# Sliding-window attention and a phase-mixing layer on one core: the first loads on other queues, later loads in smaller pieces, a shifted order list

## The chip, the cores and the metric

One core of a Trainium2 chip runs the whole kernel. The metric is the device time of one execution in microseconds (us); the time before is the median of three runs. Engines are called as the profile calls them: PE (TensorE; PEld is its weight load), DVE (VectorE), ACT (ScalarE), POOL (GpSimd), SP (SyncE).

## What is computed

Attention with 8 heads over 4 batches of 768 positions; each position sees the first 8 positions and the 96 up to itself, with a bias by distance. Then a layer over positions and channels:

```python
scores = q @ k.T / 8 - slope[h] * dist          # masked to 8 global + 96 local positions
x = softmax(scores) @ v                         # heads side by side: 768 x 512 per batch
theta = x @ w_theta
y = w_tok_r @ (x * cos(theta)) + w_tok_i @ (x * sin(theta))
u = x + y
out = u + relu(u @ w_ch)
```

Inputs and the output are fp32 in HBM; inside, the operands of matmuls are bf16.

## The kernel before, in words

**Stages of a batch.** `attention(b, p)` takes two heads (pair p of 4). It turns q and k on PE (L450, 64x64 transposes, in the plan `tk`), untangles them out of PSUM (L459) and builds a second set of keys with the global positions (`copy_s`, L465 and L466). Scores come in three groups of 3, 4 and 4 blocks of 128 columns (L496). In batch 0 the bias by distance is added on PE by a matmul with a scaled identity (L489); in later batches it is a multiplication by exp(bias) after the exponential (L513, L518). Exponentials are on ACT (L504, or L507 where a group is split over two PSUM banks); values follow (L545), the norm (L554, L555), and x is turned (L571) and copied (L574). `theta(b)` is a matmul (L620), cosine and sine on ACT (L628, L631) and a product on DVE (L637, into `zri`). `mixing(b)` multiplies by both token matrices (L662) and adds x (L671). `channel(b)` turns u (L694), multiplies by w_ch (L698), copies u (L703), adds (L720) and stores by SP's queue (L725), the last half tile by ACT's. The token matrices are turned once by `turn_w` (L589, copies L593), between theta and mixing of batch 0, and the exp(bias) tables are made on ACT after the sines of batch 0 (L746).

**Loads.** All are issued by POOL, in one chain (`load`, `chain`), and convert fp32 to bf16 on the way: for batch 0 q, k and v of two heads at a time (`piece` L354, `piece_v` L359), with the position iota (L299) between the first pair's and the second's; then w_theta (L369), w_tok_r and w_tok_i whole (L377), batch 1 in three loads of eight heads each, w_ch (L372); batches 2 and 3 again three loads each, when the buffers are free. The natural token matrix w_tok_r lies in the buffer `zri[1]` until it is turned. Eight landing semaphores go round: the ninth load waits for the first to land. `spread_v` copies v to a second layout (`vs`, L396 and L400) on POOL, ACT or DVE.

**The order.** Each step is an entry with an engine (or several, of which the plan chooses one), a planned cost, its dependencies, the PSUM banks that it takes and frees, and a priority. `Plan.order` runs a greedy model of the engines: at each moment the ready step of lowest priority goes next. PE steps of 64-row matmuls (`tiled`) and full ones are told apart, with planned costs for going from one kind to the other (`INTO`, `BACK`). `HOP` is the planned delay from one engine to the next. The steps are then issued in that order; the chip keeps the order on each engine, but its times are its own. PSUM is two double banks and four single ones.

**Keeping PE busy.** `keep_up` issues matmuls on zeros (L324): 8 and then 5 at the start, 4 after the first transposes.

Of the kernel before, what the change touches and what calls it, by code (L numbers as in the profile page):

```python
# [11 lines left out]
FP = mybir.dt.float32  # L12
# [35 lines left out]
        self.end = None  # L48


HOP = {"PE": 0.28, "ACT": 0.18, "DVE": 0.18, "POOL": 0.25, "SP": 0.0, "DMA": 1.9, "STORE": 1.5}

INTO, BACK = 0.25, 0.17

WIDER = 1.0
AHEAD = 110
# [3 lines left out]
class Plan:  # L62
# [2 lines left out]

    def __init__(self, n_wide, n_narrow):
        self.steps = []
        self.hints = []
        self.n_wide = n_wide
        self.n_tiles = n_wide + n_narrow  # L70

    def add(self, *a, **k):
        s = Step(*a, **k)
        self.steps.append(s)
        return s
# [22 lines left out]
        return best  # L98

    def order(self):  # L100

        for seed, n, width, upto in self.hints:
            draw = random.Random(seed)
            for _ in range(n):
                self.steps[draw.randrange(upto or len(self.steps))].prio += draw.uniform(-width, width)
        users = {}
        left = {}
        for s in self.steps:
# [11 lines left out]
        tiled, into = False, INTO  # L120
# [20 lines left out]
        while len(done) < len(self.steps):  # L141
# [39 lines left out]
            s.eng = eng  # L181
            if eng == "PE":
                tiled = s.tiled
                into = 0.28 if s.dense else 0.13
            s.cost, s.emit = s.ways[eng][:2]
            cost = s.cost
            if s.table and s.table != table:
# [26 lines left out]
def kernel(  # L214
# [58 lines left out]
    xT = [sb.tile([T, NP, NT, T], BF, name=f"xT_{i}") for i in range(2)]  # L273
    cs_t = [sb.tile([T, 2, 2, DM], BF, name=f"cs_{i}") for i in range(3)]
    zri = [sb.tile([T, NT, 2, DM], BF, name=f"zri_{i}") for i in range(2)]
    uT = [sb.tile([T, NP, S], BF, name=f"uT_{i}") for i in range(2)]
    un_t = [sb.tile([T, DM], BF, name=f"un_{i}") for i in range(4)]
    o_t = [sb.tile([T, DM], FP, name=f"o_{i}") for i in range(4)]
# [6 lines left out]
    ]  # L285

    plan = Plan(N_WIDE, N_NARROW)
    add = plan.add
    ANY = list(range(N_WIDE + N_NARROW - 1, -1, -1))

# [27 lines left out]
    def keep_up(n, cost, deps, prio):  # L318

        bk = Bank(False, ANY)  # L320

        def fn():
            for _ in range(n):
                nc.tensor.matmul(narrow(bk), lhsT=nought[:, 0:T], rhs=nought, start=True, stop=True)  # L324
        add("PE", n * cost, fn, deps, prio, takes=bk, frees=[bk], dense=True)

    s_nought = add("DVE", 0.2, c_nought, [], -60)
    keep_up(8, 0.43, [s_nought], -60)
    keep_up(5, 0.215, [s_nought], -59)
    s_ones = add("DVE", 0.5, c_zero, [], -50)  # L330
    s_iota = Step("POOL", 0.37, c_iota, [], -1000)
    s_ident = add("DVE", 0.12, c_ident, [s_iota], -48)
    s_dist = add("DVE", 0.9, c_dist, [s_iota], -29)
    s_W, s_I = {}, {}
    for h in range(H):
        def c_i(copy, h=h):
# [9 lines left out]
    def load(cost, fn, deps=(), issue=0.75):  # L346
        deps = list(deps) + chain[-1:] + (landed[-8:-7] if len(landed) >= 8 else [])
        i = add("POOL", issue, fn, deps, -1000)
        chain.append(i)
        landed.append(add("DMA", cost, lambda: None, [i], len(landed)))  # L350
        return landed[-1]

    def piece(src, dst, b, h0, n):
        nc.gpsimd.dma_start(  # L354
            out=dst[b % 2][:, h0:h0 + n, :, :].rearrange("p h t d -> p h (t d)"),
            in_=src[b, h0:h0 + n].rearrange("h (p t) d -> p h (t d)", p=T))

    def piece_v(b, h0, n):
        nc.gpsimd.dma_start(  # L359
            out=v_t[b % 2][:, h0:h0 + n, :, 0:D].rearrange("p h t d -> p (h t) d"),  # L360
            in_=v[b, h0:h0 + n].rearrange("h (t p) d -> p (h t) d", p=T))

    s_q, s_k, s_v, s_vs = {}, {}, {}, {}
    att_end = {}
    s_w = {}

    def weights(name):
        if name == "th":
            fn = lambda: nc.gpsimd.dma_start(out=w_th, in_=moe_w_theta.rearrange("(c p) n -> p c n", p=T))  # L369
            s_w[name] = load(2.6, fn)  # L370
        elif name == "ch":
            fn = lambda: nc.gpsimd.dma_start(out=w_ch, in_=moe_w_ch.rearrange("(c p) n -> p c n", p=T))  # L372
            s_w[name] = load(2.6, fn)
        else:
            wi = int(name)
            src = (moe_w_tok_r, moe_w_tok_i)[wi]
            fn = lambda: nc.gpsimd.dma_start(out=w_nat[wi], in_=src.rearrange("(c p) n -> p c n", p=T))  # L377
            s_w[name] = load(6.0, fn)

    def copies(eng):  # L380
        return {"POOL": nc.gpsimd.tensor_copy, "DVE": nc.vector.tensor_copy, "ACT": nc.scalar.copy}[eng]
# [1 line left out]
    def any_of(fn, deps, prio, ways, **k):  # L383

        made = {e: (c, (lambda e=e: fn(copies(e))), d) for e, (c, d) in ways.items()}
        first = next(iter(made))
        s = add(first, made[first][0], made[first][1], deps, prio, other=made, **k)
        return s
# [18 lines left out]
    def between(step):  # L407

        step.deps += chain[-1:]
        plan.steps.append(step)  # L410
        chain.append(step)

    def loads(b, h0, n, after):
        qi = load(0.5 * n, lambda: piece(q, q_t, b, h0, n), after)
        ki = load(0.5 * n, lambda: piece(k, k_t, b, h0, n), after)
        vi = load(0.8 * n, lambda: piece_v(b, h0, n), after, issue=0.62 + 0.21 * n)
        vs = spread_v(b, h0, n, [vi])
        for h in range(h0, h0 + n):
            s_q[b, h], s_k[b, h], s_v[b, h], s_vs[b, h] = qi, ki, vi, [vs[(h - h0) // 2]]

    for h in range(H):
        s_I[h] = any_of(s_I[h][0], [s_ident], s_I[h][1], {"ACT": (0.2, 0.0), "DVE": (0.12, 0.0)})
# [1 line left out]

    groups = [(0, 3), (3, 4), (7, 4)]
    po_apart = set()
    sc_apart = {(0, p, 2) for p in range(NP)}
    on_pe = {(0, p, g) for p in range(NP) for g in range(3)}
    x_done, xT_done, exp_done = {}, {}, []
    att_log = {}  # L430
# [2 lines left out]
    def attention(b, p):  # L433
# [3 lines left out]
        kS3, e3, rc = kS[n % 3], ex[n % 3], rec[n % 2]  # L437
        kq3 = kq[n % 3]
        cold = 1.1 if n == 0 else 1.0
        old = att_log.get(n - 3, [None, None])  # L440
        bank = [Bank(False, ANY), Bank(False, ANY)]

        def turn():
            for which, src in enumerate((k_t, q_t)):
                for t in range(NT):
                    for r in range(2):
                        for hh in range(2):
# [2 lines left out]
                            nc.tensor.transpose(dst[:, c0:c0 + 64],  # L450
                                                src[b % 2][64 * r:64 * r + 64, h0 + hh, t, :],
                                                ident[64 * r:64 * r + 64, 64 * r:64 * r + 64])
        tk = add("PE", 0.4, turn, [s_k[b, h0], s_q[b, h0], s_ident, old[0]], pr + 10, takes=bank, tiled=True)
        if n == 0:
            keep_up(4, 0.215, [tk], 0)

# [5 lines left out]
        def copy_s(copy):  # L462
# [1 line left out]
            inner = inner.rearrange("p (r s) -> p r s", r=2)[:, :, 0:2 * T].rearrange("p r (t a) -> p r t a", t=2)  # L464
            copy(out=kS3.rearrange("p (r t) a -> p r t a", r=2)[:, :, :, G:T], in_=inner[:, :, :, G:T])  # L465
            copy(out=kS3[:, :, 0:G], in_=kq3[:, 0, 0:1, 0:G].to_broadcast([T, NT - 2, G]))  # L466
        both = {"DVE": (0.87, 0.0), "ACT": (0.72, 0.0)} if b or p < 1 else {"DVE": (0.87, 0.0)}
        kq0 = any_of(lambda copy: untangle(0, copy), [tk, old[0]], pr + 12, both, frees=bank[0:1])
        kq1 = any_of(lambda copy: untangle(1, copy), [tk, old[0]], pr + 12, both, frees=bank[1:2])
        cS = any_of(copy_s, [kq0, kq1], pr + 13, {"DVE": (0.5, 0.0), "ACT": (0.85, 0.1)})  # L470

        mult = []
        for g, (c0, n_c) in enumerate(groups):
            apart = (b, p, g) in sc_apart
            sc = [Bank(False, ANY), Bank(False, ANY)] if apart else [Bank(True, ANY)]
# [41 lines left out]
                    w = w[:, :, None, :].to_broadcast([T, 2, 2, 2 * T])  # L517
                    nc.vector.tensor_mul(dst, dst, w)  # L518
            need = [old[1]] + ([kq0] if g == 0 else [kq0, kq1, cS]) + ([s_dist, s_I[h0], s_I[h0 + 1]] if by_pe else [])
            s1 = add("PE", (0.057 + 0.107 * by_pe) * n_c * cold, scores, need, pr + 20 + g, takes=sc, tiled=True)  # L520
            s2 = add("ACT", 0.13 * len(sc) + 2 * n_c * T * 0.00076, exps, [s1, old[1]], pr + 30 + g, table="exp", frees=sc)
            if by_pe:
                s3 = s2
            else:
                s3 = add("DVE", 0.12 + 2 * n_c * T / 1960.0, weigh, [s2, s_W[h0], s_W[h0 + 1]], pr + 40 + g)
            mult.append(s3)
            last_s = s1

            exp_done.append(s2)

# [19 lines left out]
        def norm():  # L550
# [5 lines left out]
            else:  # L556
                for hh in range(2):
# [1 line left out]
                    nc.vector.reciprocal(rc[:, hh, :], ps[:, :, D])  # L559
                    nc.vector.tensor_mul(dst[:, hh, :, :], ps[:, :, 0:D],  # L560
                                         rc[:, hh, :, None].to_broadcast([T, NT, D]))
        att_log[n] = [last_s, last]
        nm = add("DVE", 0.85 + 0.3 * len(po), norm, [last] + [z_done[b - 2, st] for st in range(NT) if b >= 2], pr + 60, frees=po)
        x_done[b, p] = nm

# [7 lines left out]
        def copy_x(copy):  # L573
# [1 line left out]
                 in_=narrow(bk).bitcast(BF)[:, 0:S])  # L575
        t1 = add("PE", 0.34, turn_x, [nm], pr + 70, takes=bk)
        xT_done[b, p] = any_of(copy_x, [t1] + mix_log.get(b - 2, []), pr + 71,
                               {"DVE": (0.5, 0.0), "ACT": (0.7, 0.0)} if b or p == 3 else {"DVE": (0.5, 0.0)}, frees=[bk])
        att_end[b, p] = last

    def turn_w(wi, prio):
        got = []
        for st in range(NT):
            bk = Bank(False, ANY)

            def fn(st=st, bk=bk):
                ps = narrow(bk).bitcast(BF)
                for tt in range(NT):
                    nc.tensor.transpose(ps[:, tt * T:(tt + 1) * T],  # L589
                                        w_nat[wi][:, tt, st * T:(st + 1) * T], ident)  # L590

            def cp(copy, st=st, bk=bk):
                copy(out=wT[wi][:, st, :], in_=narrow(bk).bitcast(BF)[:, 0:S])  # L593
            t1 = add("PE", 0.35, fn, [s_w[str(wi)], s_ident], prio + st, takes=bk)
            got.append(any_of(cp, [t1], prio + st, {"DVE": (0.5, 0.0), "ACT": (0.72, 0.0)}, frees=[bk]))
        return got

# [130 lines left out]
            o_log.append(st)  # L728


    for h0 in (0, 2, 4, 6):
        loads(0, h0, 2, [])
        if h0 == 0:
            between(s_iota)
    weights("th")
    weights("0")
    weights("1")
    loads(1, 0, 8, [])
    weights("ch")
    for p in range(NP):  # L740
        attention(0, p)
# [9 lines left out]
    channel(0)  # L751
    for b in range(1, B):
        if b >= 2:
            loads(b, 0, 8, [att_end[b - 2, p] for p in range(NP)])
        for p in range(NP):
            attention(b, p)
        theta(b)
        mixing(b)
        channel(b)
# [38 lines left out]
```

## Time and profile before

| | us |
|---|---|
| median of three runs (lowest to highest) | 182.67 (182.27 to 183.24) |
| the profiled execution | 181.96 |
| its span | 180.0 |
| PE busy in the span | 167.9 |
| DVE, ACT, POOL busy | 124.2, 122.8, 35.9 |
| DMA queue of POOL: packets, MB | 35728, 12.85 |

The span goes from the first to the last instruction of the profiled execution; the rest of its time lies around it. Busy time counts instructions that run, so an engine's idle time in a stretch is the stretch less its busy time. The time from a load's issue to its landing is in the part on DMA issues: 5.6 and 6.4 us in the middle for q and k of two heads (192 KB in bf16), 21.7 and 24.1 us for eight heads (768 KB), 14.8 and 19.6 us for the token matrices (1152 KB).

### The profile page before, as it was taken

What the parts mean: (1) busy time and instruction counts of PE and PEld (TensorE: products, weight loads), DVE (VectorE), ACT (ScalarE), POOL (GpSimd) and SP (SyncE); (2) the same over time, 40 slices, a digit from 0 to 9 for tenths busy, and PEclk for the clock granted to TensorE, in tenths of its full rate; (3) what the DMA queues carried; (4) which work ended last, traced back from release to release, by engine and by line L of the source; (5) the groups of instructions that cost most, each with busy time, mean ns of one, the idle gap of its engine ahead of it and who ended that gap; (6) DMA issues with size and microseconds to landing.
All of it is one profiled execution on the core that took longest, in us unless ns stands there. A gap on an engine that the chain in (4) does not pass through costs nothing.

```text
span 180.0 us, 5292 instructions
## 1 busy us (share of the span) xinstructions
PE 167.9 (93%) x2311; PEld 101.6 (56%) x2325; DVE 124.2 (69%) x231; ACT 122.8 (68%) x189; POOL 35.9 (20%) x44
## 2 busy tenths in 40 slices
PE   7977979989699999999999999999999999999991
PEld 2434454766367666455666664656566555555560
DVE  1757955867898897788999964678679356524352
ACT  2697786999886885998979939948686990203010
POOL 7996930040530164006000000000000000000000
PEclk9999999999999999999999999999999999999998
DMA  4999999999999959992000210031001300400404
GB/s 55 144 179 185 210 210 209 204 187 150 203 204 165 191 81 207 179 182 100 4 0 4 108 71 2 4 134 46 0 4 58 117 4 0 162 13 4 174 0 175
DMA packets 39350, 19.47 MB, mean 108 GB/s; under 512 B 25376, under 2 KB 36384, under 8 KB 39328
## 3 DMA queue, kind: packets, MB, share of 16 engines
q0 software_dynamic: 35728, 12.85, 70.0%
q1 hardware_dynamic: 3456, 6.16, 9.5%
q8 instruction: 18, 0.29, 0.7%
q10 hardware_dynamic: 144, 0.13, 0.2%
q14 instruction: 4, 0.03, 0.1%
HBM read 25.69 MB, written 6.29 MB: 178 GB/s over the span
## 4 chain that ended last, share of the span: by engine, by line
PE 78%; ACT 7%; DMA 4%; POOL 3%; issue 3%; DVE 2%; DVEq 0%; POOLq 0%; ACTq 0%
PE ps L662 34%; PE ps L698 11%; PE ps L620 9%; PE ps L496 6%; PE ps L545 6%; DMA k<-in_k_dram 4%; PE ps L450 3%; PE ps L694 3%; PE ps L571 3%; ACT cs L628 2%; ACT ex L504 2%; PE ps L489 1%; POOL q L354 1%; POOL v L359 1%; ACT cs L631 1%
## 5 line engine op out<-in xcount | busy, mean ns | idle before, releaser
L662 PE MATMUL ps<-wT,zri 128*128 128x384 bf16 x384 | 69.1, 326 | 0.0
L662 PEld LDWEIGHTS <-zri 128*128 128x128 bf16 x384 | 35.1, 98 | 22.8 <-issue 0.9
L504 ACT ACTIVATE ex<-ps 128x1024 bf16<-128x1024 f32 (+1 forms) x44 | 40.5, 953 | 7.4 <-PE ps L496 7.3
L671 DVE TENSOR_TENSOR uT<-xT,ps 128x384 bf16<-128x384 bf16 x32 | 17.6, 551 | 17.8 <-PE ps L662 17.7
L703 ACT COPY un<-ps 128x512 bf16<-128x512 bf16 x18 | 10.7, 595 | 26.1 <-PE ps L694 26.0
L637 DVE TENSOR_TENSOR zri<-x,cs 128x1024 bf16<-128x1024 bf16 x24 | 16.5, 695 | 11.2 <-ACT cs L631 11.2
L698 PE MATMUL ps<-w_ch,uT 128*128 128x512 bf16 (+1 forms) x91 | 23.4, 370 | 0.5 <-issue 0.2
L459 DVE COPY kq<-ps 128x768 bf16<-128x768 bf16 x20 | 18.8, 952 | 5.5 <-PE ps L450 5.3
L620 PE MATMUL ps<-w_th,xT 128*128 128x512 bf16 x92 | 21.4, 379 | 0.2
L628 ACT ACTIVATE cs<-ps,halfpi 128x512 bf16<-128x512 f32 x24 | 17.4, 723 | 5.5 <-PE ps L620 5.4
L720 DVE SCALAR_TENSOR_TENSOR o<-ps,un 128x512 f32<-128x512 f32 (+1 forms) x25 | 16.6, 668 | 4.8 <-PE ps L698 4.4
L518 DVE TENSOR_TENSOR ex<-ex,Wm 128x1024 bf16<-128x1024 bf16 x24 | 16.5, 686 | 1.7 <-ACT ex L504 1.7
L545 PEld LDWEIGHTS <-ex 128*128 128x128 bf16 x352 | 13.7, 97 | 4.1 <-DVE ex L518 0.7
L496 PE MATMUL ps<-kq 64*128 64x128 bf16 (+1 forms) x192 | 15.1, 226 | 0.7 <-ACT ex L504 0.5
L555 DVE TENSOR_TENSOR x<-ps,rec 128x768 bf16<-128x768 f32 x16 | 15.3, 957 | 0.6
L620 PEld LDWEIGHTS <-xT 128*128 128x128 bf16 x96 | 9.2, 98 | 10.9 <-DVE xT L574 0.5
L545 PE MATMUL ps<-v,ex 128*128 128x65 bf16 x224 | 15.3, 193 | 0.0
L631 ACT ACTIVATE cs<-ps 128x512 bf16<-128x512 f32 x24 | 15.3, 638 | 0.0
L359 POOL DMA_DIRECT2D v<-in_v_dram x7 | 10.9, 1560 | 15.9 <-ACT wT L593 13.2
L574 ACT COPY xT<-ps 128x768 bf16<-128x768 bf16 x10 | 8.0, 799 | 7.8 <-PE ps L571 7.7
L396 POOL COPY vs<-v 128x520 bf16<-128x520 bf16 x9 | 6.4, 732 | 30.1 <-DMA v<-in_v_dram 30.1
L698 PEld LDWEIGHTS <-uT 128*128 128x128 bf16 x100 | 8.8, 98 | 6.1
(68 smaller groups left out, 207.0 us busy)
## 6 DMA issues: line engine op xcount, KB each, us to landing
out_dram<-o SPq DMA_DIRECT2D x23, 256.0 KB, 2.1
q<-in_q_dram POOLq DMA_DIRECT2D x3, 768.0 KB, 21.7
k<-in_k_dram POOLq DMA_DIRECT2D x3, 768.0 KB, 24.1
v<-in_v_dram POOLq DMA_DIRECT2D x3, 768.0 KB, 25.4
zri<-in_moe_w_tok_r_dram POOLq DMA_DIRECT2D x1, 1152.0 KB, 14.8
w_nat<-in_moe_w_tok_i_dram POOLq DMA_DIRECT2D x1, 1152.0 KB, 19.6
q<-in_q_dram POOLq DMA_DIRECT2D x4, 192.0 KB, 5.6
k<-in_k_dram POOLq DMA_DIRECT2D x4, 192.0 KB, 6.4
```

What stands on the lines that cost most here:

```text
L459: copy(out=kq3[:, r, :, :].rearrange("p w (a t) -> p w a t", t=NT), in_=ps.rearrange("p (w t a) -> p w a t", w=2, t=NT))
L496: nc.tensor.matmul(ps[hh][:, col * T:(col + w) * T], lhsT=lhsT, rhs=kq3[R, i // 3, 1, i % 3 * T:(i % 3 + w) * T], start=not by_pe, stop=no ...
L504: nc.scalar.activation(dst, wide(sc[0])[:, :, 0:n_c * T], AF.Exp, scale=scale)
L518: nc.vector.tensor_mul(dst, dst, w)
L545: nc.tensor.matmul(dst, lhsT=l, rhs=r, start=(i == 0), stop=(i == len(mms) - 1))
L620: nc.tensor.matmul(tiles()[:, i, :], lhsT=xT[b % 2][:, p, st + i, :], rhs=w_th[:, p, :], start=(p == 0), stop=(p == NP - 1))
L628: nc.scalar.activation(cs[:, 0, 0:per, :], tiles(), AF.Sin, bias=halfpi)
L631: nc.scalar.activation(cs[:, 1, 0:per, :], tiles(), AF.Sin)
L662: nc.tensor.matmul(narrow(bk)[:, 0:nt * T], lhsT=zri[b % 2][:, st, wi, c * T:(c + 1) * T], rhs=wT[wi][:, st, cols], start=(k + i == 0), st ...
L671: nc.vector.tensor_add(uT[b % 2][:, c, cols], xT[b % 2][:, c, n0:n0 + nt, :].rearrange("p t c -> p (t c)"), narrow(bk)[:, 0:nt * T])
L698: nc.tensor.matmul(narrow(bks[hf])[:, 0:wide_n], lhsT=uT[b % 2][:, c, tt * T:(tt + 1) * T], rhs=w_ch[:, c, hf * wide_n:(hf + 1) * wide_n], ...
L720: nc.vector.scalar_tensor_tensor(o[:, cols], in0=narrow(bks[hf])[:, 0:cols.stop - cols.start], scalar=0.0, in1=un[:, cols], op0=ALU.max, o ...
```

## The change

The first pair's q and k no longer go through POOL. SP issues k and ACT issues q, in fp32, into space in `zri[0]` that is free at that time, and one copy each (DVE or ACT, as the plan chooses) casts them to bf16. The iota goes ahead of all of POOL's loads, and the first pair's v goes behind the second pair's q and k. The token matrices are loaded in two halves of columns each; the transposes of a half wait for that half alone. Batches 1 to 3 are loaded in two lots of four heads for q and k, and v in pieces of two heads. The five later dummy matmuls at the start are gone. In batch 0, group 1 of the scores is split over two banks instead of group 2, and the untangling copies and x copies of all pairs may go to ACT. Planned costs and delays have other values. Last, the priorities of 77 steps are shifted by given amounts; which steps these are follows from their number in the list.

```diff
-HOP = {"PE": 0.28, "ACT": 0.18, "DVE": 0.18, "POOL": 0.25, "SP": 0.0, "DMA": 1.9, "STORE": 1.5}
+HOP = {"PE": 0.28, "ACT": 0.18, "DVE": 0.18, "POOL": 0.25, "SP": 0.0, "DMA": 1.6, "STORE": 1.5}
-INTO, BACK = 0.25, 0.17
+INTO, BACK = 0.25, 0.145
...
+        for i, by in self.shifts.items():
+            self.steps[i].prio += by
...
-                into = 0.28 if s.dense else 0.13
+                into = 0.25 if s.dense else 0.13
...
+    first_t = zri[0].rearrange("p a b c -> p (a b c)").bitcast(FP)[:, 0:4 * NT * D]
+    first_t = first_t.rearrange("p (w h c) -> p w h c", w=2, h=2)
...
+    plan.shifts = {
+        33: -69, 35: -117, 87: -339, 101: 229, 179: 235, 180: -69, 194: -97, 198: -22, 202: -5, 203: 24,
...
     keep_up(8, 0.43, [s_nought], -60)
-    keep_up(5, 0.215, [s_nought], -59)
...
-    s_dist = add("DVE", 0.9, c_dist, [s_iota], -29)
+    s_dist = add("DVE", 1.4, c_dist, [s_iota], -29)
...
-            fn = lambda: nc.gpsimd.dma_start(out=w_nat[wi], in_=src.rearrange("(c p) n -> p c n", p=T))
-            s_w[name] = load(6.0, fn)
+            for i in range(w_parts):
+                cols = slice(i * S // w_parts, (i + 1) * S // w_parts)
+                fn = lambda cols=cols: nc.gpsimd.dma_start(out=w_nat[wi][:, :, cols],
+                                                           in_=src.rearrange("(c p) n -> p c n", p=T)[:, :, cols])
+                s_w[name, i] = load(5.6 / w_parts, fn)
...
+    def first_pair():
+
+        got = []
+        for which, (src, dst) in enumerate(((k, k_t), (q, q_t))):
+            def fn(src=src, which=which, eng=(nc.sync, nc.scalar)[which]):
+                eng.dma_start(out=first_t[:, which], in_=src[0, 0:2].rearrange("h (p t) d -> p h (t d)", p=T))
+
+            def cast(copy, dst=dst, which=which):
+                copy(out=dst[0][:, 0:2, :, :].rearrange("p h t d -> p h (t d)"), in_=first_t[:, which])
+            i = add(("SP", "ACT")[which], 0.4, fn, [], -2000)
+            at = add("DMA", 1.0, lambda: None, [i], -1000)
+            got.append(any_of(cast, [at], -100, {"DVE": (0.85, 0.0), "ACT": (0.75, 0.0)}))
+        for h in (0, 1):
+            s_k[0, h], s_q[0, h] = got
+
+    def load_v(b, h0, n, after):
+        for h1 in range(h0, h0 + n, 2):
+            vi = load((0.78 if b else 0.86) * 2, lambda h1=h1: piece_v(b, h1, 2), after, issue=1.04)
+            vs = spread_v(b, h1, 2, [vi])
+            for h in (h1, h1 + 1):
+                s_v[b, h], s_vs[b, h] = vi, vs
...
+        if (b, h0) == (0, 0):
+            first_pair()
+            return
...
+        if (b, h0) == (0, 2):
+            load_v(0, 0, 2, [])
+        load_v(b, h0, n, after)
...
-    sc_apart = {(0, p, 2) for p in range(NP)}
+    sc_apart = {(0, p, 1) for p in range(NP)}
...
-        both = {"DVE": (0.87, 0.0), "ACT": (0.72, 0.0)} if b or p < 1 else {"DVE": (0.87, 0.0)}
+        both = {"DVE": (0.87, 0.0), "ACT": (0.72, 0.0)}
...
-            s1 = add("PE", (0.057 + 0.107 * by_pe) * n_c * cold, scores, need, pr + 20 + g, takes=sc, tiled=True)
+            s1 = add("PE", (0.0455 + 0.142 * by_pe) * n_c * cold, scores, need, pr + 20 + g, takes=sc, tiled=True)
...
-                               {"DVE": (0.5, 0.0), "ACT": (0.7, 0.0)} if b or p == 3 else {"DVE": (0.5, 0.0)}, frees=[bk])
+                               {"DVE": (0.5, 0.0), "ACT": (0.7, 0.0)}, frees=[bk])
...
-            t1 = add("PE", 0.35, fn, [s_w[str(wi)], s_ident], prio + st, takes=bk)
+            t1 = add("PE", 0.35, fn, [s_w[str(wi), st * w_parts // NT], s_ident], prio + st, takes=bk)
...
+    between(s_iota)
     for h0 in (0, 2, 4, 6):
         loads(0, h0, 2, [])
-        if h0 == 0:
-            between(s_iota)
...
-    loads(1, 0, 8, [])
+    for h0 in (0, 4):
+        loads(1, h0, 4, [])
...
-            loads(b, 0, 8, [att_end[b - 2, p] for p in range(NP)])
+            for h0 in (0, 4):
+                loads(b, h0, 4, [att_end[b - 2, p] for p in (h0 // 2, h0 // 2 + 1)])
```

## The prediction

> **What bounds the kernel now.** I read the chain of waits first, then TensorE's idle time by stage, then the places where it idles. The chain of the whole span, in order of time (start, length, what; "issue" is time for which the profile shows no cause):
>
> ```profile
> 7.46 7.22 DMA k<-in_k_dram
> 14.73 0.58 PE ps L450 x48
> ...
> 28.68 0.69 ACT cs L628
> ...
> 35.19 1.40 ACT wT L593 x2
> ...
> 47.77 1.00 issue
> 48.77 0.50 PE ps L450 x38
> ```
>
> Up to 14.73 the chain is POOL's row of load issues and then one load, pair 2's k; from there to 48.77 it goes to and fro between TensorE, ScalarE and VectorE; after 48.77 it is TensorE alone, up to the tail (last matmuls, one eviction, one store). The same by stage (start:end, length, then busy time of each engine):
>
> ```profile
> 5.88:14.73 8.85, 6.67 (x166) 3.48 (x166) 5.54 (x13) 7.33 (x12) 8.18 (x10) 1.00 1.67 165
> 14.73:27.44 12.71, 10.88 (x249) 6.60 (x250) 9.20 (x16) 9.00 (x14) 8.29 (x9) 1.00 1.33 204
> 27.44:37.96 10.52, 9.79 (x98) 6.40 (x97) 7.25 (x14) 9.26 (x16) 0.90 (x1) 1.00 1.26 206
> 37.96:48.77 10.81, 9.28 (x218) 5.53 (x215) 7.64 (x18) 10.80 (x18) 3.32 (x4) 1.00 2.31 174
> 48.77:175.13 126.36, 125.53 (x1570) 77.25 (x1582) 91.21 (x159) 83.42 (x125) 10.52 (x12) 1.00 0.54 80
> ```
>
> Length minus the first busy time is TensorE's idle time: 2.18, 1.83, 0.73, 1.53 and 0.83 us. So the kernel is 5.88 us before the first transpose, 6.3 us of idle in the next 43, and then 126 us in which TensorE never waits. A microsecond won before 48.77 comes through to the end; the later part changes only with TensorE's own work. Where it idles, from the timeline (start, busy, instruction, idle before it and what ended it):
>
> ```profile
> 10.54 0.38 PE L450 MATMUL ps<-ident,k 64*64 64x64 bf16 x24 [0.78 <-DMA k<-in_k_dram]
> 14.73 0.38 PE L450 MATMUL ps<-ident,k 64*64 64x64 bf16 x24 [0.86 <-DMA k<-in_k_dram]
> 25.96 0.51 PE L571 MATMUL ps<-ident,x 128*128 128x128 bf16 x6 [0.64 <-DVE x L555]
> 27.09 0.51 PE L571 MATMUL ps<-ident,x 128*128 128x128 bf16 x6 [0.62 <-DVE x L555]
> 36.63 1.50 PE L589 MATMUL ps<-ident,w_nat 128*128 128x128 bf16 x24 [0.56 <-ACT wT L593]
> 48.77 0.31 PE L450 MATMUL ps<-ident,k 64*64 64x64 bf16 x14 [1.00 <-issue]
> ```
>
> Two waits for k, two for the last norms of batch 0, one for a weight copy, and one pause inside a step that nothing explains.
>
> **Part by part.**
>
> *First pair on SP and ACT.* POOL loses two issues (0.82 and 0.72), the iota (0.37) goes ahead of all loads, so q of pair 1 is issued at 1.26 + 0.37 = 1.63 instead of 4.22. V of pair 0 moves behind q, k of pair 1: 1.63 + 0.72 + 0.72 = 3.07 instead of 2.80; it lands at 7.86 now, its value matmuls run at 11.04, so 0.3 us there is covered by 3. K of pair 1 landed 5.6 us after its issue, in a queue behind three other loads; with none ahead on its own queue I expect what pair 0's k took (issue 2.08, landed 5.84: 3.8), so about 6.1 instead of 10.5. From there the traced spacings of landings, less the two pieces taken out, put pair 2's k at about 12.3 instead of 14.68. TensorE was ready for it at 13.87 (14.73 less 0.86); 0.78 and about 0.4 earlier is 12.7, so both k waits go: 1.64 us. Next late is VectorE's untangling copy of pair 1 (0.95 each, two in a row from 11.17, VectorE idle 2.95 before); earlier data let it start earlier, ACT may now take it too (0.80), and it shares the 0.2 us waits that follow. I count **2.0** of the 4.0 us of idle in the first two stages, bounds 0.5 and 2.8.
>
> *When the first transpose starts.* No load by SP or ACT is in the trace. Nearest rows: their stores, 256 KB in 2.1 us and 128 KB in 1.9, so 0.2 for 128 KB more. The two loads are 768 KB in fp32: 1.9 + 5 x 0.2 = 2.9 us at that pace; at the loads' own 200 GB/s, 786 KB take 3.9 and the sum is 5.8. I take 3.9, nearer the stores, whose rows go by the same two queues. SP and ACT start at 0.74 (ACT's first row), so they land at 4.6 (3.6 to 6.5). Then the new casts, VectorE for one and ACT for the other, side by side; the nearest rows are the 768-column copies, 0.96 and 0.80, with about 0.15 on either side: transposes at 5.8 (4.8 to 7.7) against 5.88. I count **0**, from +1.0 to -1.8. The issue itself (0.33 on SP, 0.37 on ACT) has nothing ahead of it: the table loads of 1.28 us stand directly before the instructions that need them wherever else the trace has one (24.99, 37.30), so I expect it behind the issue; ahead of it the landing is 1.3 later.
>
> *Five dummy matmuls less.* They ran from 4.6 to 5.7, where TensorE waits anyway. 0, apart from the clock (below).
>
> *Weights in halves.* The first token matrix landed at 27.15 whole; its first half comes 2.8 earlier (its 5.6 us halved), and the stream is some 2 us earlier. So its transposes (0.35 a step) can lie in the 1.26 us before theta, where TensorE now has nothing else. I count half, **0.6** (0 to 1.2).
>
> *Batch 1 in pieces of 4 and 2 heads.* The first two pairs' k comes after 4 heads of q and 4 of k, not 8 and 8: about 35 instead of 40.49, their v about 38 instead of 46.7. The 2.26 us of idle from 27.44 to 48.77 is in a stretch where ACT is busy 20.1 of 21.3 us, so only what ACT's work has to do with data coming late can go. **0.7** (0 to 1.5).
>
> The price: POOL issues 4 q/k of 0.8 and 4 v of 1.04 a batch, 7.4 us, instead of 0.88 + 0.88 + 2.22 = 4.0. With the weights' halves that is 12 us more on an engine busy 36 of 180. Behind an issue on POOL stand its copies for vs, and the value matmuls wait for these. An issue may itself wait: the ninth load waits for the first one's landing (0.91 at 14.97), one waited 13.18, and nothing came of it. 0, up to 0.8. In bytes, pieces of 192 KB land 1.06 apart, a quarter of the 3.84 of a 768 KB load is 0.96: a tenth dearer, in a stream that runs ahead.
>
> The Trainium skill, "DMA: Bandwidth & Descriptors", Bandwidth, speaks against this part: it wants loads of a MiB or more, and its section on one DMA's anatomy gives each a fixed 2 us. By that as an estimate the seven more pieces up to batch 1's last v would cost 14 us of stream. This trace's 1.06 us between landings shows the fixed part overlapped, so I don't count it.
>
> *Split of the scores* (group 1 on two banks, not group 2): exps 2 x 0.53 instead of 1.02, in the one place as in the other: 0.
>
> *77 shifts and the plan's constants* add and remove no instruction; they change the order. Four sit on landings of loads, which issue nothing. After 48.77 TensorE changes 27 times into 64-row matmuls and back, a pair of changes costing 0.19 (starts of neighbouring matmuls less their columns at full clock): 5 us in all. With TensorE never waiting there, the only gain left is fewer changes, the loss more of them or a new wait. **0**, within 0.6. Orders that come out of a plan don't fit the chip exactly: I take **-0.2** for it.
>
> **Sum:** 2.0 + 0 + 0.6 + 0.7 + 0 - 0.2 = 3.1 us. The profiled execution took 181.96 (span 180.0 and 1.96 around it), which gives 178.9. The three timed runs have their median 0.71 above it, at 182.67; carried over, **179.6**.
>
> **Rivals.**
>
> *The stream of loads sets the pace (0.18).* The order of bytes is the same, and fp32 shares the engines that carry it. DMA is full from 4.5 to 63 us (page, part 2). If w_tok_i still lands at 32.8, its transposes (34.91 now) hold the mixing where it is, and all won before is waited out; only the 0.7 stays: 182.0. For it: 206 GB/s throughout. Against it: the stream starts 2.6 us earlier for pair 1, and at 32.8 TensorE was 2 us behind the landing.
>
> *The clock isn't released (0.09), which ends slower.* The first dummies start 0.43 apart, from 4.58 on 0.21: the clock doubled there, after eight (the granted-clock row doesn't show it). Thirteen kept TensorE busy to 5.7, eight end at 4.6. If the release misses them, pairs 0 and 1 run at half speed. Columns of one pair: 1.2 us of position matmuls, 0.9 of scores, 0.5 of transposes, 0.7 of values, so 3.3 more a pair, less some 1.1 that hides in waits. One pair slow gives 181.8, two 184.0; it turns slower when the half clock lasts beyond about 12 us. Against it: in the trace eight sufficed.
>
> By the Trainium skill, "TensorE: Matmul & The Clock Gate", Part 1, the release needs one busy window of about 3.4 us, free-running, so a run can just miss it. Eight dummies, 8 x 0.43 = 3.4, are exactly one such window; by that rule this rival would come in some runs and not in others, and the after times would scatter. The trace agrees as far as the 3.4 us before its release go.
>
> *The new order waits where the old one didn't (0.13).* TensorE's queue is in order; a step put first whose input is late holds all behind it. At the 2% of the page's better early stages instead of 0.7%, the last 126 us cost 1.8 more, and eight pairs of changes 1.5: 182.9; double that, 186. Against it: the new constants for scores (0.18 for eight matmuls) with the entry of 0.25 still lie above the 0.33 that the chain shows.
>
> *More (0.04):* all upper ends, 175 to 176.5.
>
> The forecast (2 to 5.5 won) keeps 0.56. About 0.5% (0.9 us) is what a measurement of this kernel tells from no change. Faster: 0.56 + 0.04 + half of the stream's + 0.02 + 0.02 = 0.73; same 0.12; slower 0.15 (clock 0.07, order 0.08). Range: below, 2.8 + 0.5 + 1.2 + 1.5 = 6.0, 176.7; above, 183.2, which takes in the stream, the slow single pair and the cheaper order.
>
> **What would show it.** Right: k waits at L450 gone for pairs 1 and 2; first transpose at 5.5 to 6; w_tok_r's first transposes before theta; theta's first matmul at about 25 (27.44 now); TensorE's idle before 49 at 3 us; its stage after that as long as now. Wrong: first transpose after 7; w_tok_i landing at 32.8 or later; 0.43 us between full matmuls after 5 us; idle in the last 126 us above 2.

## The result and the profile after

The changed kernel takes 184.81 us in the median of four runs (184.25 to 185.39), against 182.6 for the kernel before beside it: a ratio of 1.0117 (1.0075 to 1.0159), so 1.2% slower. The profiled execution took 184.93, its span is 183.2.

By stage (start:end, length, busy time of PE, PEld, DVE, ACT, POOL, clock, DMA share, GB/s), the first four rows lie about where the first four of before lay:

```profile
5.75:14.00 8.25, 6.91 (x200) 3.77 (x200) 5.42 (x11) 5.32 (x8) 7.32 (x9) 1.00 1.82 176
14.00:26.40 12.40, 11.40 (x226) 7.14 (x224) 8.44 (x21) 11.41 (x18) 5.10 (x6) 1.00 1.42 200
26.40:37.00 10.60, 10.44 (x140) 6.85 (x141) 8.23 (x16) 10.18 (x18) 4.10 (x5) 1.00 1.57 192
37.00:48.00 11.00, 10.93 (x255) 6.93 (x254) 10.17 (x21) 10.84 (x17) 7.88 (x11) 1.00 1.58 193
48.00:69.70 21.70, 21.63 (x264) 13.19 (x263) 15.05 (x27) 18.04 (x28) 11.41 (x15) 1.00 1.71 192
69.70:80.00 10.30, 5.25 (x26) 2.35 (x24) 5.89 (x12) 4.84 (x9) 1.97 (x3) 0.68 0.73 93
80.00:177.70 97.70, 97.70 (x1204) 59.96 (x1202) 66.71 (x120) 57.03 (x83) 0.32 (x1) 1.00 0.14 50
```

Length less PE's busy time, up to 48 us, is 1.34 + 1.00 + 0.16 + 0.07 = 2.6 us of idle, where it was 6.3: by the profile the start has won 3.7 us. From 80 on PE never waits. All of the loss lies in one row, 69.7 to 80, with 5.05 us idle and a mean clock of 0.68. The two rows of the page for PE and its clock, 4.6 us to a digit, show the same place at a glance:

```profile
PE   7779889999999992699999999999999999999991
PEclk9999999999999999579999999999999999999999
```

In the timeline of the changed kernel, that place reads (start, busy, engine, line, what, idle before and what ended it):

```profile
72.83 0.30 DVE L409 COPY vs<-v 128x520 bf16<-128x520 bf16 x1 [8.53 <-DMA v<-in_v_dram]
...
73.37 1.27 DVE L677 TENSOR_TENSOR zri<-x,cs 128x1024 bf16<-128x1024 bf16 x2
74.14 0.69 ACT L668 ACTIVATE cs<-ps,halfpi 128x512 bf16<-128x512 f32 x1 [6.26 <-DVE zri L677]
74.57 0.41 DVE L743 COPY un<-ps 128x512 bf16<-128x512 bf16 x1
...
75.03 1.87 PE L738 MATMUL ps<-w_ch,uT 128*128 128x512 bf16 x4 [5.05 <-DVE un L743]
```

Read it from the top: DVE stands 8.5 us at one copy, whose v hasn't landed. Behind it in DVE's queue are the products of theta (ACT waits 6.3 us for them, since its three buffers are full) and a copy that frees a PSUM bank, for which PE waits 5.05 us. Then four matmuls of 512 columns take 1.87 us, where four of the same line take 1.03 at 68.73, before the stop.

That v belongs to batch 3, heads 4 and 5, and its value matmuls are planned for 122 us. Why is its copy at 64? One of the 77 shifts is 651: -187, and step 651 is this load's landing. It issues nothing, but the plan serves the landings that wait for the DMA in order of priority, and with -187 it served this one ahead of five loads that were issued before it. The kernel's own plan, in its own time:

```
step 651  landing of v, batch 3, heads 4 and 5   priority -149   planned 61.08 to 62.64
step 637  landing of k, batch 3, heads 0 to 3    priority   33   planned 62.64 to 64.60
step 652  its copy to vs, on DVE                                 planned at 64.24
```

On the chip all 40 loads of POOL's queue landed in the order of issue, and this one at 72.73 (issued at 59.81, 12.9 us to landing).

### The profile page after: what moved, and what is told of

Same layout as the page of the kernel before. It is cut to its first block, busy times and chain, and to the rows that moved or that the text cites. A ratio compares the mean times of both kernels' runs of the same rounds, so it can differ in the third digit from the quotient of the medians.

```text
span 183.2 us, 5343 instructions
## 1 busy us (share of the span) xinstructions
PE 169.3 (92%) x2320; PEld 101.9 (56%) x2320; DVE 124.9 (68%) x239; ACT 121.8 (66%) x185; POOL 43.0 (23%) x57
## 4 chain that ended last, share of the span: by engine, by line
PE 60%; ACT 12%; DMA 11%; DVE 11%; POOL 3%; issue 2%; DVEq 0%; POOLq 0%; ACTq 0%
PE ps L702 27%; PE ps L738 11%; DMA v<-in_v_dram 7%; PE ps L660 6%; ACT ex L544 5%; PE ps L536 5%; DMA k<-in_k_dram 4%; PE ps L585 3%; PE ps L734 3%; PE ps L490 2%; PE ps L611 2%; DVE kq L499 2%; DVE zri L677 2%; ACT cs L668 1%; DVE x L595 1%
## 5 line engine op out<-in xcount | busy, mean ns | idle before, releaser
L702 PE MATMUL ps<-wT,zri 128*128 128x384 bf16 x384 | 70.6, 327 | 0.0
L702 PEld LDWEIGHTS <-zri 128*128 128x128 bf16 x384 | 34.5, 98 | 22.0 <-issue 0.6
L738 PE MATMUL ps<-w_ch,uT 128*128 128x512 bf16 (+1 forms) x100 | 26.0, 394 | 5.0 <-DVE un L743 5.0
L743 ACT COPY un<-ps 128x512 bf16<-128x512 bf16 x14 | 8.2, 584 | 25.6 <-PE ps L734 21.5
L668 ACT ACTIVATE cs<-ps,halfpi 128x512 bf16<-128x512 f32 x24 | 16.9, 706 | 9.2 <-DVE zri L677 6.3
L368 POOL DMA_DIRECT2D v<-in_v_dram x16 | 16.4, 1026 | 11.1 <-DMA w_nat<-in_moe_w_tok_i_dram 3.6
L499 DVE COPY kq<-ps 128x768 bf16<-128x768 bf16 x16 | 15.1, 951 | 3.2 <-PE ps L490 3.2
L738 PEld LDWEIGHTS <-uT 128*128 128x128 bf16 x100 | 9.5, 102 | 13.5 <-issue 6.9
L671 ACT ACTIVATE cs<-ps 128x512 bf16<-128x512 f32 x24 | 14.5, 616 | 0.0
L499 ACT COPY kq<-ps 128x768 bf16<-128x768 bf16 x16 | 12.7, 815 | 2.2 <-PE ps L490 2.2
```

What stands on the lines that cost most here:

```text
L499: copy(out=kq3[:, r, :, :].rearrange("p w (a t) -> p w a t", t=NT), in_=ps.rearrange("p (w t a) -> p w a t", w=2, t=NT))
L668: nc.scalar.activation(cs[:, 0, 0:per, :], tiles(), AF.Sin, bias=halfpi)
L702: nc.tensor.matmul(narrow(bk)[:, 0:nt * T], lhsT=zri[b % 2][:, st, wi, c * T:(c + 1) * T], rhs=wT[wi][:, st, cols], start=(k + i == 0), st ...
L738: nc.tensor.matmul(narrow(bks[hf])[:, 0:wide_n], lhsT=uT[b % 2][:, c, tt * T:(tt + 1) * T], rhs=w_ch[:, c, hf * wide_n:(hf + 1) * wide_n], ...
```

## Experiments

**Is it that shift?** Four kernels on one chip; the kernel before had a median of 183.0 beside them.

```diff
 order = plan.order()
+late = plan.steps[652:654]
+order = [s for s in order if s not in late]
+at = next(i for i, s in enumerate(order) if s.start >= 77.9)
+order[at:at] = late
```

> The changed kernel with its own order, but the two copies to vs of batch 3's third pair (v, heads 4 and 5) put later on the one engine that has them, VectorE; TensorE, ScalarE, GpSimd and SyncE keep every instruction in its place. Theory (the shift on a landing made the plan believe that this v lands 10 us before it does, so VectorE stood 8.5 us at it with everything behind it): TensorE's stop of 5.05 us at 70 goes, and with it the half clock after it (some 2.2 us); 184.8 less 7.2 is 177.6. Rival (the order is too tight in many places, and the next late input takes its place): 181 to 184, with a stop of several us near 70 to 80 still there.

Measured: 178.45 (178.36 to 179.57), ratio to the kernel before 0.977 (0.9728 to 0.9811). The stop is gone:

```profile
69.70:80.00 10.30, 10.11 (x228) 6.31 (x231) 9.36 (x17) 10.11 (x16) 1.84 (x3) 1.00 0.92 170
```

Two DVE instructions, put elsewhere with all else in its place, are worth 6.4 us. The theory holds, and this kernel beats both.

```diff
-        582: 231, 586: 118, ..., 651: -187, 665: -27,
+        582: 231, 586: 118, ..., 665: -27,
```

> The changed kernel without one of its 77 shifts, the one of -187 on the landing of v of batch 3, heads 4 and 5; the plan is made anew with the other 76. Theory: no stop at 70, 177 to 179.5 (the order is no longer the one that the other shifts belong to). Rival (the stop comes from the order as a whole): above 182.

Measured: 178.84 (177.9 to 179.76), ratio 0.9777. One number in a list of 77, with the order that the plan makes of the other 76, is the difference between a slower and a faster kernel.

```diff
-    plan.shifts = { ... }
+    plan.shifts = {}
```

> The changed kernel with no shifts at all: the new loads and constants alone. Theory (the new loads bring the gain, the shifts brought the loss): 178 to 180.5, no stop over 2 us. Rival (the shifts bring what gain there is): 182 to 184.

Measured: 184.25 (184.06 to 185.67), ratio 1.008 (1.0045 to 1.0115). Here my theory was wrong: the loads and constants alone, in the order that the plan makes without shifts, bring nothing. PE has no wait for a late load, but it pauses in the middle of a step, without any wait (1.3 us at 46, 2.3 us at 59), and the second pause is followed by half clock from 61.3 to 64.7. That is the profile of an execution of 185.67 us.

```diff
-landed.append(add("DMA", cost, lambda: None, [i], len(landed)))
+landed.append(add("DMA", cost, lambda: None, [i] + landed[-1:], len(landed)))
```

> The changed kernel with all 77 shifts, but in the plan each landing comes after the one before it, as POOL's queue issues them, so that the four shifts on landings have no say. Theory: no wait for a load of more than 2 us on VectorE, 177 to 179.5. Rival (these four shifts are not the cause): above 182, with a stop as long as now.

Measured: 182.63 (182.37 to 183.5, and one execution at 186.05), ratio 0.9986 (0.9957 to 1.0015). No wait for a load over 2 us on DVE and no stop at 70, as expected, but the time of 177 to 179.5 was missed: the order is another one, and it has waits of its own on PE: 1.1 us for DVE at 11, 1.1 for w_tok_i at 28, a pause of 1.3 at 57.8. So the other shifts don't carry over to every order: in this one they bring no gain, in that of e2_drop_one, made anew as well, they do.

**What are the new queues and the pieces worth?** Both on e1_move_two, with every other instruction in its place; the kernel before had 182.98 beside them.

```diff
-eng.dma_start(out=first_t[:, which], in_=src[0, 0:2]...)
+piece(src, (k_t, q_t)[which], 0, 0, 2)      # on POOL, and no casts
```

> The kernel with the two copies moved (e1_move_two, 178.45), in which only the first pair's q and k go back to GpSimd's queue with the cast on the way, ahead of all else there; no casts on VectorE and ScalarE; all other instructions in their order. Theory (the other queues are worth what pair 1's and pair 2's loads gain by them): first transposes at about 5.9 as now, k of pair 1 some 2 us later, 1 to 2.5 us lost: 179.5 to 181. Rival (the pieces behind it, which run ahead of their use, give all of the gain): within 0.7 of 178.45.

Measured: 179.85 (179.32 to 180.85), ratio 0.9821. By the medians the first pair by SP and ACT is worth 1.4 us, by the ratios (0.9821 and 0.977, whose intervals overlap) 0.9: about 1 us is all that can be said. The first pair's q lands at 6.53, 1.3 later, and pair 2's k at 14.09, 2.0 later than in e1_move_two; PE waits for it:

```profile
14.13 0.38 PE L490 MATMUL ps<-ident,k 64*64 64x64 bf16 x24 [1.71 <-DMA k<-in_k_dram]
```

```diff
+(token matrices: the first half's step loads both, the second none;
+ batch 1: q, k, v of eight heads where the first piece stood, none at the others)
```

> The kernel with the two copies moved (e1_move_two, 178.45), in which the token matrices come whole and batch 1 in three loads of eight heads, each issued where its first piece was; all else in its order. The order was made for pieces, so TensorE now waits where it counts on them. Theory (pieces are worth the earlier landing of w_tok_r's half and of batch 1's first k): 1.5 to 4 us lost, 180 to 182.5, with waits of TensorE for w_tok_r near 26 and for k near 36. Rival (the stream runs so far ahead that pieces don't matter): within 0.7 of 178.45.

Measured: 187.66 (186.28 to 188.14), ratio 1.0232: 9.2 us lost, more than twice what I had as the upper end. PE waits 1.9 us for w_tok_r at 24, then 3.7 us at 44 for DVE, with half clock after each (25.7 to 29.1 and 46.2 to 53.0). The wait for k that I had near 36 is 0.4 us at 39. The one at 44 is the stop at 70 once more: ACT stands 4.8 us at a copy of batch 1's v, which lands whole at 45.31, and DVE as long at the copy behind it. The price is that of whole loads under an order made for pieces; what a plan made for whole loads would lose wasn't tried.

**The pauses.** In the kernels so far the longest pauses of PE without a wait came after 446 of its instructions (e1_move_two), 1469 (before), 1466 and 1975 (e3_no_shifts) and 1977 (e4_in_turn), counting the weight loads and matmuls of the trace, which lacks a few: distances of about 512 and 1024, in quite different steps.

```diff
+if n == 8:
+    for _ in range(12):
+        nc.tensor.matmul(narrow(bk)[:, 0:16], lhsT=nought[:, 0:T], rhs=nought[:, 0:16], start=True, stop=True)
```

> The kernel without shifts (e3_no_shifts, 184.25), with 12 matmuls of 16 columns on zeros more after the first eight dummies, so 24 more instructions in TensorE's stream, in time that it waits anyway; order of all else the same. In three kernels TensorE paused without any wait, always at about its instruction 447, 1470 or 1977 (distances of 512 and 1024). Theory (the pause belongs to a place in the instruction stream, as when the next block of instructions is late): the pause of 2.3 us that lies after the third q transpose of a step at 59 comes 24 instructions earlier in the work, after 15 of the k transposes of that step, or in another length there; 183 to 185. Rival (it belongs to that step or to what else runs then): it stays after the third q transpose.

Measured: 183.22 (182.01 to 183.95), ratio 1.0005. The same step in e3_no_shifts, then here:

```profile
58.77 0.38 PE L481 MATMUL ps<-ident,k 64*64 64x64 bf16 x24
58.99 0.20 PE L481 MATMUL ps<-ident,q 64*64 64x64 bf16 x3
61.48 0.53 PE L481 MATMUL ps<-ident,q 64*64 64x64 bf16 x21 [2.30 <-issue]
```

```profile
59.10 0.32 PE L484 MATMUL ps<-ident,k 64*64 64x64 bf16 x15
59.83 0.28 PE L484 MATMUL ps<-ident,k 64*64 64x64 bf16 x9 [0.41 <-issue]
```

The pause moved from behind the 27th transpose of the step to behind the 15th, by the 24 instructions put in, to the instruction. So did the one at 46: there four values after the transposes, here (46.79) behind the 16th of the 24 q transposes, again twelve matmuls earlier. The pauses belong to the stream, not to the work. The one at 59 is shorter here, and the half clock after it is gone; this profile has a half clock of its own at 15, after 1.8 us of idle time in two pieces. The profile's DMA part has 18 packets of 16 KB on a queue called "instruction" for these 4651 weight loads and matmuls, some 258 to a packet:

```profile
q8 instruction: 18, 0.29, 0.7%
```

The times of these packets show what the pause is. Counting pauses from 0.35 us on, the twelve traces have 13, after 446, 702, 1466 to 1469, 1721 or 1975 to 1977 instructions, so about 256 or a multiple apart; and each of the 13 ends 1.3 to 1.65 us after such a packet has been read. The pause of 2.3 us ends at 61.48, its packet at 59.96; that of 1.0 us in the kernel before ends at 48.77, its packet at 47.36. At the other places of this spacing PE gets there a microsecond or more after the packet, and stops for less than 0.35 us or not at all. So by these times it waits for a block of instructions. Why the block is late was not tried: all pauses lie before the last load has landed, which fits packets that queue behind loads, but their own time, some 1 us, is no longer then than later.

**The half clock after the stop.**

```diff
+if s is plan.steps[245]:                     # the matmuls that stop
+    for _ in range(23):
+        nc.tensor.matmul(PS[0][:, 1, :], lhsT=nought[:, 0:T], rhs=nought, start=True, stop=True)
 s.emit()
```

> The changed kernel with its stop at 70, and 23 matmuls of 512 columns on zeros put in TensorE's queue just ahead of the one that stops (some 5 us of work on a free half of a bank). Theory (the half clock after the stop comes from TensorE idling for 5 us, and costs some 2 us): the stop stays as long, matmuls after it start 0.22 apart, 182.3 to 183.3. Rival (the half clock comes from elsewhere): 184.5 to 185.5, matmuls 0.43 apart after it.

Measured: 182.7 (182.4 to 183.71), ratio 0.9978. The stop is as long (DVE stands 8.5 us again), and the same four matmuls, which took 1.87 us, now take

```profile
75.24 1.02 PE L738 MATMUL ps<-w_ch,uT 128*128 128x512 bf16 x4
```

So of what the shift cost, 2.1 us is the half clock that follows an idle PE, and the rest the stop itself.

**The dummies at the start.** In the profile of e1_move_two the clock came late:

```profile
6.95 1.49 PE L334 MATMUL ps<-nought 128*128 128x512 bf16 x3 [0.34 <-issue]
```

Three matmuls 0.43 apart, where the kernel before has three in 0.81; by the trace's clock record it was full from 9.03 on. Of the nine profiles with eight dummies, e3_no_shifts has it as late (10.05); the other seven have it between 3.86 and 5.51.

```diff
-            for _ in range(n):
+            for _ in range(13 if n == 8 else n):
```

> The kernel with the two copies moved (e1_move_two), with thirteen dummy matmuls at the start again instead of eight, all else in its order. In the profiled execution of e1_move_two the dummies still start 0.43 apart at 7 us, so the clock there came later than in the execution before the change (4.7). Theory (eight sometimes miss the release, thirteen don't): clock full by 6 us in the profile, the median 0.3 to 1.2 below that of the same kernel with eight, run beside it, and less scatter. Rival (it doesn't matter, since the first pair waits for VectorE and ScalarE anyway, or the five more hold up the first transposes): no difference, or up to 0.6 slower.

> The kernel with the two copies moved (e1_move_two) once more, beside the one with thirteen dummies: 178 to 179.

Measured, in five rounds: 178.66 (178.36 to 180.13) with thirteen and 178.45 (178.18 to 180.0) with eight. No difference: the rival holds. The second profile of the kernel with eight has its full clock from 5.5, 3.5 us earlier, and the same span of 176.7. In that one PE waits 1.8 us for pair 2's k, so what the clock had cost would have been waiting anyway. Thirteen didn't give the full clock by 6 us, as my theory had it, but at 6.51, and they end at 6.78, so that the first transposes come 0.9 us later than with eight:

```profile
1.19 5.59 PE L334 MATMUL ps<-nought 128*128 128x512 bf16 x13 [1.19 <-DVE nought L326]
6.71 0.38 PE L490 MATMUL ps<-ident,k 64*64 64x64 bf16 x24
```

That profile is of an execution of 180.13 us.

## Why the prediction was wrong, step by step

**The first pair.** Transposes were forecast for 5.8 and came at 5.75; the loads landed at 4.84 and 5.24, forecast 4.6, and casts of 0.83 and 0.77 us, shorter than forecast, made up for it. Pair 1's k landed at 7.79, not 6.1: I had let it run as if alone, beside 768 KB of fp32. Pair 2's k, forecast for 12.3, landed at 12.27. PE waited 1.15 us for it. Two more shifts, 33 and 35, sit on the landings of this q and k: the plan puts both ahead of the landing of pair 1's v, which was issued before them, and has this k at 8.4. With the landings in turn (e4_in_turn) PE has no wait for it, but that is another order, so the cause isn't shown. Idle in the first two stages went from 4.0 to 2.34: 1.7 us, for a forecast of 2.6, the 2.0 of this term and the 0.6 of the weights. The waits for the last norms, 1.26 in the kernel before, are 0.51 now, which is the weights' part; so 0.9 is left for the 2.0 here. The term was twice too large, and e5_first_by_pool, with about 1 us, says the same.

**The pieces.** From 26.4 to 48 the idle time is 0.23, from 2.26 before: 2.0 us for 0.7. That is more luck than forecast: 1.0 of it is the pause at 48.77 of the kernel before, a late block of instructions that the profile of the changed kernel happens to lack, and 0.56 the wait for a weight copy at 36.63; 0.5 is left. The transposes of w_tok_r's halves do lie between the last norms, and theta's first matmul comes at 27.84, not at the 25 that I named:

```profile
25.31 0.33 PE L629 MATMUL ps<-ident,zri 128*128 128x128 bf16 x3
...
26.49 0.51 PE L611 MATMUL ps<-ident,x 128*128 128x128 bf16 x6 [0.51 <-DVE x L595]
26.83 1.17 PE L629 MATMUL ps<-ident,zri 128*128 128x128 bf16 x18
27.84 1.46 PE L660 MATMUL ps<-w_th,xT 128*128 128x512 bf16 x6
```

The small loads cost no stream: batch 1's last v landed at 45.42, before the change at 46.70. The fixed 2 us a load of the Trainium skill, "DMA: Bandwidth & Descriptors", section on the anatomy of one DMA, are hidden here, as the 1.06 us between landings had said.

**The step that failed** is the one on the shifts: "Four sit on landings of loads, which issue nothing", put at 0 within 0.6, with 0.2 taken off for an order that doesn't fit the chip. One of the four cost 6.4 us by e1_move_two. That they issue nothing is true. But a landing's place in the plan decides where the plan puts what waits for it, and the chip's queue knows nothing of priorities. I had counted a list of numbers by what they emit, and not by what they make the plan believe. Looking up what step 651 is, and that POOL's queue can't let it pass, would have shown it. The rival that it belongs to, a new order that waits where the old one didn't, had the right mechanism, but on another engine: I looked at TensorE's queue, and it was VectorE's that stood at a late input. I priced it as a spread of small waits, and it was one stop of 5.05 us and 2.1 us of half clock; the sign that I gave for it, idle above 2 us in the last 126, is what came.

**The rest of the shifts** I also put at 0, since PE never waited after 48. Without them (e3_no_shifts) the kernel takes 184.25, with them and without the stop 178.45: 5.8 us, so this half of the term failed too, the other way. Where they come from is open. The two profiles are 7.2 us apart; pauses (4.0 us in three, against one of 1.0) and the half clock in e3_no_shifts are some 4.6 of that. But neither is the work of a shift as such, and three of the seven executions of e3_no_shifts had a mean clock of 1.00 and still took 184.06 to 184.34.

**The sum** of 3.1 us, to 179.6, was near for the kernel that I thought I saw: without the stop it is 178.45, 4.6 below the 183.0 beside it. That is luck. The loads and constants, for which I had 3.3 us, bring a loss of 1.2 in an order without shifts, and the shifts, for which I had nothing, bring 5.8.

**The other rivals.** The stream didn't hold the pace: w_tok_i landed at 31.93, 0.8 earlier, and PE had no wait for it. The clock did come late with eight dummies in two profiles of nine, as the Trainium skill's free-running window, "TensorE: Matmul & The Clock Gate", Part 1, has it; in e1_move_two it cost nothing, since a load was later still. My price of 2.2 us for one slow pair took off only 1.1 for such cover.

## What to carry to other kernels

In an order that a model makes, a late input costs what stands behind it on an in-order queue, not the step that waits: here a copy needed 50 us later stopped three engines. Check a planned order against the one thing that the model bent and the chip didn't, the order of a DMA queue: in all twelve traces POOL's loads landed in the order of issue, and a plan in which one passes another is wrong about whatever waits for it. And a long stop of PE is paid twice: here 5.05 us of idle time and 2.1 us for the half clock after it.

## What the runs showed of the hardware

- The half clock comes in stretches of 3.41 us or twice that (6.83 after the 5.05 us stop), by the trace's clock record. It took less than such a stretch of idle time: in e2_drop_one 1.8 us of idle in 2.1, then half clock 1.4 us later, though PE was busy by then:

```profile
10.60:12.70 2.10, 0.29 (x16) 0.17 (x16) 0.98 (x3) 1.05 (x2) 1.50 (x3) 1.00 1.93 175
12.70:14.10 1.40, 1.40 (x59) 0.83 (x60) 0.84 (x1) 0.80 (x1) 1.11 (x2) 1.00 1.39 202
14.10:17.50 3.40, 3.40 (x26) 1.19 (x25) 2.50 (x8) 2.73 (x5) 2.32 (x3) 0.50 1.70 187
```

  The 1.8 us of idle at 10.8 in the second profile of e1_move_two brought no half clock. What decides can be worked out from the twelve traces: cut the time into windows of 3.41 us from the moment of the first full clock, and add up PE's idle time in each. Full clock was followed by half clock after every window with 1.62 us of idle time or more (1.62 in e7_more_instructions, 1.71 in e5_first_by_pool, 1.81 in e2_drop_one) and after none with 1.58 or less. Half clock was followed by full clock after windows with at most 0.75 us, and not after 0.82 (the start of e1_move_two) or more. The 1.8 us that cost nothing lay across two windows, with 1.53 of idle time in one; the 5.05 us stop filled one and left 1.52 in the next, which kept the clock at half. The Trainium skill, "TensorE: Matmul & The Clock Gate", Part 1, names an idle window of about 3.4 us for the fall; these runs have the same window, and show the fall with half of it idle.
- Much of the scatter of one kernel goes with such a stretch: of the kernel before, 24 executions with a mean clock of 0.995 or more took 181.74 to 183.04, and 22 with 0.991 or less took 182.94 to 184.99.
- PE pauses of 0.35 to 2.3 us stand at fixed places of its instruction stream, about 256 instructions or a multiple apart, while loads run. Each ends 1.3 to 1.65 us after a 16 KB packet on the instruction queue. Twelve matmuls more ahead of them move them by twelve matmuls. They don't come in each execution: one profile of e1_move_two has one at 15 us, the other none.
- The loads by SP and ACT, 384 KB each and side by side, took 4.1 and 4.5 us from issue to landing. The first packets of POOL's casting loads come at 4.3 us, though the first of these was issued at 1.36; alone, in the kernel before, it was issued at 1.26 and landed at 4.74, here at 6.37.
